# A recurrent attention followed by two mixtures on one core: seven token blocks instead of eight in the first mixture, a bit-narrowing in two passes, sums moved between engines, and a new order of the first steps

## The chip, the cores and the metric

The kernel runs on 1 core of a Trainium2 chip. The metric is the device time of the program in microseconds (us): the median of several runs, and beside it the time of one profiled execution, whose trace is read here. TensorE (PE in the profile) multiplies matrices, VectorE (DVE), ScalarE (ACT) and GpSimd (POOL) work element by element, and SyncE (SP) issues the DMAs. Each engine works through its own list of instructions in order; semaphores hold an instruction back until what it needs is there.

## The reference

```python
for t in range(S):                                   # 4 batches, 8 heads, S = 768, D = 48
    cur = np.einsum('bhd,bhe->bhde', u[None] * kt, vt)
    y[:, :, t] = np.einsum('bhd,bhde->bhe', rt, state + cur)
    state = wt[:, :, :, None] * state + np.einsum('bhd,bhe->bhde', kt, vt)
x = y as (3072 tokens, 384)
h = x @ w_in;  g = h * sigmoid(1.702 h);  x = g @ w_out          # first mixture, 384 -> 2048 -> 384
h = x @ w_in2; s = h * softmax(h)                                # second mixture, 384 -> 1024 -> 384
out = (layer_norm(s) * g_ln) @ w_out2
```

The weights of both mixtures arrive as 64-bit floats and are made 32-bit floats on the chip. Every product of a mixture is made of three matrix multiplications (high times high, high times low part, low times high), each at the short float format of the PE.

## The kernel before

The 3072 tokens are 24 units of 128. A unit's attention is a chain over several engines: cumulative products of the decays on DVE (`f_scan`, then `f_back`), scaled r and k (`f_r0` and `f_k` on DVE, `f_r1` on POOL), scores on PE (`scores`), a mask on DVE (`masked`), the new state on PE and DVE (`states`, `update`), the result on PE (`mix`), the bonus term (`bonus` on POOL, `bonus_sum`, then `bonus_mul` on POOL), the sum with it (`total`), and the turned copy that the mixture reads, as a high and a low part (`turn`, `out_hi`, `out_lo`). Each unit needs the state of the one before it.

The first mixture goes over blocks of units (`BLOCKS`) and over 16 slices f of its hidden size. A slice of a block is a rise (`rise`, 9 multiplications of 128x128 weights with all tokens of the block), two gelus on ACT (`gelu`), a low part on DVE (`rest`) and a fall (`fall`, 9 multiplications into three accumulators). A multiplication streams 128 columns for each unit of the block. The results of a rise stand in two banks of PSUM by turns, and a bank is free again after the block's `rest`.

The weights of slice f are loaded raw (`load1`), narrowed from 64 to 32 bits in passes by `narrow` (one on ACT, the others on DVE), and split into a high and a low part (`split1`). The weights of the second mixture are narrowed by the same function beside the last block.

The order of everything up to the third or fourth block is written out by hand in `START`, a string of tokens that is worked through from left to right. In it `F1` to `F5` are the first steps of a unit, `SA`, `M0`, `M1`, `DA`, `DB`, `D`, `U1`, `U2` scores, masks, states and updates, `B` the bonus products, `BR` its sum, `BV` its product, `X`, `V`, `T`, `O`, `OL` the result, its sum, its turning and its two parts; `N0` to `N3` the passes of the narrowing, `H` and `C` the split of a weight slice; `h`, `e`, `g`, `o` rise, gelu, rest and fall of block and slice. A star puts a step that DVE would do on PE and ACT (for `V`, `OL` and `C`: PE subtracts or adds through a multiplication with the unit matrix, ACT copies). After START the tables `VISITS`, `ENTRY`, `SHORT` and `LONG` say at which slice of which block the remaining units' steps are issued. From unit `LONE` on, a unit's result is turned by two trips through DRAM instead of by PE. In the end the second mixture goes over units; `xsplit` makes the two parts of a unit's input.

Of the kernel before, what the change touches and what calls it, by code (L numbers as in the profile page):

```python
# [46 lines left out]
V:2* g0:1 N3:3 Lw:6 C:2* N1:4 h0:2 T:2 F5:3 N2:4 H:3 C:3 La:3 N0:5 N1:5 o0:0 O:2 h0:3 e0:2 N3:4 Lw:7 ST:3 N2:5 F1:4
g0:2 BR:3 OL:2* SA:3 M1:3 SK:3 e0:3 DA:3 U1:3* o0:2 M0:3 DB:3 F2:4 g0:3 H:4 C:4 N0:6 La:4 N0:7 U2:3* N1:6 N3:5 N2:6
N1:7 Lrkw:5 BV:3 X:3* Lb:4 N3:6 h0:4 V:3* Lw:8 T:3 O:3 e0:4 H:5 o0:1 N2:7 OL:3* g0:4 o0:3 Lw:9 h1:0 e1:0 F3:4 N3:7
h1:1 F5:4 o0:4 g1:0 F4:4 Lw:10 N0:8 Ln:4 C:5 H:6 N1:8 e1:1 g1:1 N0:9 N1:9 C:6 H:7 C:7 o1:0 h1:2 N2:9 e1:2 SA:4 g1:2  # L50
ST:4 h1:3 e1:3 U2:5 SK:4 o1:1 h1:4 B:4 g1:3 N3:9 o1:3 Lw:12 N0:10 M1:4 M0:4 e1:4 g1:4 N1:10 h0:5 Lrkw:6 N2:8 N2:10
BR:4 BV:4 N3:10 e0:5 g0:5 o1:4 h1:5 e1:5 g1:5 D:4 o1:2 N0:12 h1:6 U1:4 e1:6 o0:5 H:9 H:10 h1:7 N3:8 Lw:11 Lw:13 X:4
g1:6 Lb:5 Ln:5 N1:12 F1:6 H:8 o1:6 h0:6 e1:7 N2:12 e0:6 g1:7 h0:7 N0:11 o1:7 e0:7 o1:5 U2:4 F4:6 N3:12 g0:6 o0:6 F1:5
C:8 g0:7 h1:8 e1:8 h0:8 e0:8 V:4 T:4 F2:6 F2:5 C:9 o0:7 O:4 g1:8 h0:9 F3:5 OL:4 La:5 g0:8 N1:11 e0:9 g0:9 C:10 Lw:15
N2:11 F5:5 H:12 o1:8 h1:9 h0:10 N3:11 e1:9 g1:9 o0:8 e0:10 o0:9 C:12 g0:10 N0:13 ST:5 H:11 o1:9 SK:5 N1:13 h1:10 e1:10
C:11 Lw:14 h0:11 N2:13 g1:10 F4:5 B:5 F3:6 o0:10 N0:14 N1:14 h0:12 SA:5 e0:12 e0:11 N3:13 g0:11 g0:12 N2:14 N0:15 D:5
# [13 lines left out]
VISITS = (1, 6, 10, 14, 18, 22, 26) + tuple(range(32, 64, 4))  # L70
# [3 lines left out]
    "nat+3 r0+2",  # L74
    "states+1 v2+2 updates+1 place+2 scan+3 back+3 k+3 sendk+3",
    "hi lo",
)
SHORT = (
    "scores+1 states+1 mix rk+3 total send v+2 v2+2 vd+1 fetch masks+1 w+4",
    "updates+1 r1+2 sum+1 bonus+2",  # L80
    "mul+1 nat+3 place+2 r0+2 scan+3",
    "back+3 k+3 sendk+3",
# [900 lines left out]
```

## Time and profile before

| | |
|---|---|
| median of 3 runs | 709.71 us (709.21 to 710.52) |
| profiled execution, its own time | 710.13 us |
| span from the first to the last instruction in it | 708.4 us |
| busy in the span: PE, DVE, ACT, POOL | 687.4, 553.1, 304.5, 145.4 us |
| granted clock of PE | 1.0 of full speed in all 40 slices of the span |
| first rise of block 0; first rise of block 3 (the first of three units) | 36.98 us; 174.29 us |

Busy time of PE is that of a pipeline: it shows that PE had work in flight, not that it ran at its peak. How fast it goes is read from the starts of one multiplication after the other, so in the chain that ended last as a piece's length over its number of multiplications. The profiled execution is 0.42 us above the median of the runs.

### The profile page before, as it was taken

How to read it: one execution, taken by the hardware profiler on the slowest of the kernel's cores; microseconds unless marked ns; L12 is line 12 of the kernel's file. 1: busy time of each engine (PE TensorE's matmuls, PEld its weight loads, DVE VectorE, ACT ScalarE, POOL GpSimd, SP SyncE). 2: the span in 40 equal slices, each digit the busy share in tenths (PEclk: the TensorE clock that was granted, in tenths of full speed). 3: DMA queues.
4: the chain of work that ended last, by engine and by line, in shares of the span. 5: the costliest groups of instructions: out<-in, count | busy, mean ns of one | idle time of the engine just before them, and what ended most of it. 6: DMA issues, size and time to landing. Idle time of an engine off the chain costs nothing.

```text
span 708.4 us, 16384 instructions
## 1 busy us (share of the span) xinstructions
PE 687.4 (97%) x6541; PEld 614.1 (87%) x6541; DVE 553.1 (78%) x898; ACT 304.5 (43%) x617; POOL 145.4 (21%) x144
## 2 busy tenths in 40 slices
PE   2899999999999999999999999999999999999997
PEld 2678999999999999988878888888889979999997
DVE  8799999888899999577777532687688878888872
ACT  2356554433233333323333223556655554545552
POOL 5431322343223232122322100120000000000000
PEclk9999999999999999999999999999999999999999
DMA  7668533433456567544444212332145544444443
GB/s 267 243 201 261 179 132 107 143 86 113 132 147 193 154 166 209 169 120 120 123 146 124 85 34 80 101 108 68 60 147 161 166 153 159 142 142 155 156 146 112
DMA packets 69292, 101.11 MB, mean 143 GB/s; under 512 B 15840, under 2 KB 53984, under 8 KB 69216
## 3 DMA queue, kind: packets, MB, share of 16 engines
q1 hardware_dynamic: 69072, 99.97, 45.9%
q8 instruction: 51, 0.84, 0.5%
q14 instruction: 25, 0.20, 0.1%
q10 hardware_dynamic: 144, 0.10, 0.0%
HBM read 76.38 MB, written 23.66 MB: 141 GB/s over the span
## 4 chain that ended last, share of the span: by engine, by line
PE 91%; DVE 3%; DMA 2%; ACT 1%; issue 1%; SPq 1%; ACTq 0%; DVEq 0%
PE acc L622 27%; PE h L597 27%; PE o L733 14%; PE right L665 8%; PE left L665 6%; PE att L364 2%; PE att L274 1%; PE att L365 1%; DMA yd<-x2b 1%; PE d L519 1%; DVE w L192 1%; PE att L235 1%; DVE P L171 1%; PE att L267 1%; PE att L395 0%
## 5 line engine op out<-in xcount | busy, mean ns | idle before, releaser
L622 PE MATMUL acc<-gh,w 128*128 128x256 f32 (+2 forms) x768 | 210.7, 339 | 0.0
L597 PE MATMUL h<-xTh,w 128*128 128x256 f32 (+2 forms) x768 | 173.7, 337 | 0.0
L605 ACT ACTIVATE gh<-h 128x256 fp32r<-128x256 f32 (+2 forms) x128 | 62.8, 491 | 228.8 <-PE h L597 220.5
L622 PEld LDWEIGHTS acc<-gh,w 128*128 128x128 f32 x768 | 136.5, 189 | 12.4
L597 PEld LDWEIGHTS h<-xTh,w 128*128 128x128 f32 x768 | 128.4, 189 | 12.0 <-ACT w L521 0.5
L622 PE MATMUL acc<-gl,w 128*128 128x256 f32 (+2 forms) x384 | 128.9, 336 | 0.0
L612 DVE TENSOR_TENSOR gl<-h,gh 128x256 fp32r<-128x256 f32 (+2 forms) x128 | 70.5, 552 | 72.7 <-ACT h L607 71.5
L597 PE MATMUL h<-xTl,w 128*128 128x256 f32 (+2 forms) x384 | 87.5, 336 | 0.1
L622 PEld LDWEIGHTS acc<-gl,w 128*128 128x128 f32 x384 | 72.7, 189 | 5.5
L733 PE MATMUL o<-w,qh 128*128 128x384 f32 x384 | 70.9, 336 | 0.0
L597 PEld LDWEIGHTS h<-xTl,w 128*128 128x128 f32 x384 | 64.7, 189 | 6.2 <-DVE xTl L415 0.5
L733 PEld LDWEIGHTS o<-w,qh 128*128 128x128 f32 x384 | 67.7, 188 | 1.6
L607 ACT ACTIVATE h<-h 128x256 f32<-128x256 f32 (+2 forms) x128 | 62.4, 488 | 0.0
L710 POOL TENSOR_TENSOR sm<-sm,mhalf 128x1 f32<-128x1 f32 x24 | 13.2, 549 | 200.3 <-DVE sm L709 187.1
L177 POOL TENSOR_TENSOR R<-rk,P 64x512 f32<-64x512 f32 x24 | 31.2, 1302 | 89.4 <-PE att L365 45.8
L665 PE MATMUL right<-w,x2h 128*128 128x512 f32 x156 | 40.0, 392 | 0.9 <-ACT x2h L653 0.9
L206 POOL TENSOR_TENSOR nr<-nr,nk 128x384 f32<-128x384 f32 x24 | 29.3, 1219 | 52.0 <-DMA nk<-in_nat 51.8
L286 DVE TENSOR_TENSOR R<-att,cc 64x256 f32<-64x256 f32 (+1 forms) x82 | 36.8, 448 | 1.2 <-PE att L277 0.2
L224 POOL TENSOR_TENSOR vd<-vd,dg 128x384 f32<-128x384 f32 x14 | 14.0, 1001 | 114.4 <-DMA vd<-in_vn 55.1
L733 PE MATMUL o<-w,ql 128*128 128x384 f32 x192 | 37.1, 334 | 0.0
L665 PEld LDWEIGHTS right<-w,x2h 128*128 128x128 f32 x156 | 29.1, 188 | 6.8 <-ACT x2h L653 1.2
L665 PE MATMUL left<-w,x2h 128*128 128x512 f32 x132 | 33.8, 392 | 0.0
(192 smaller groups left out, 1222.6 us busy)
## 6 DMA issues: line engine op xcount, KB each, us to landing
rk<-in_rkw SPq DMA_DIRECT2D x24, 512.0 KB, 4.2
d<-t SPq DMA_DIRECT2D x24, 512.0 KB, 2.6
back<-d SPq DMA_DIRECT2D x96, 128.0 KB, 2.9
x2b<-in_w SPq DMA_DIRECT2D x11, 768.0 KB, 5.7
w<-in_rkw SPq DMA_DIRECT2D x24, 261.0 KB, 3.1
nr<-in_nat SPq DMA_DIRECT2D x24, 192.0 KB, 3.1
nk<-in_nat SPq DMA_DIRECT2D x24, 192.0 KB, 3.0
vs<-in_vn SPq DMA_DIRECT2D x48, 96.0 KB, 4.1
```

Source lines behind the costliest of these rows:

```text
L177: (e or self.nc.gpsimd).tensor_tensor(out=heads(R1[0:64]), in0=heads(s["rkw"][0:64, 0:HC]), in1=heads(s["P"])[0:64, :, 0:C], op=ALU.mult)
L206: g.tensor_tensor(out=s["nr"], in0=s["nr"], in1=s["nk"], op=ALU.mult)
L224: nc.gpsimd.tensor_tensor(out=heads(s["vd"]), in0=heads(s["vd"]), in1=dg.unsqueeze(2).to_broadcast([128, H, D]), op=ALU.mult)
L286: self.nc.vector.tensor_tensor(out=heads(R[q:q + 64])[:, h:h + n], in0=a, in1=m.unsqueeze(1).to_broadcast([64, n, C]), op=ALU.mult)
L364: mm(out=y[h][t:t + 32], lhsT=s["R0"][0:112, w], rhs=s["vs0"][0:112, e], start=one, stop=one or h == 7, tile_position=(0, t))
L597: nc.tensor.matmul(out=h_ps, lhsT=W1[f][:, ws + c * 128:ws + (c + 1) * 128], rhs=xs[:, c, tok], start=n == 0, stop=n == 8)
L605: nc.scalar.activation(out=gh, in_=h_ps, func=AF.Gelu_apprx_sigmoid)
L607: return nc.scalar.activation(out=h_ps, in_=h_ps, func=AF.Gelu_apprx_sigmoid)
L612: nc.vector.tensor_tensor(out=gl_, in0=g, in1=gh.bitcast(F32), op=ALU.subtract)
L622: nc.tensor.matmul(out=a, lhsT=W1[f][:, ws + e * 128:ws + (e + 1) * 128], rhs=gs, start=first and n == 0, stop=last and n == 2)
L665: nc.tensor.matmul(out=h_ps[:, b * 512:(b + 1) * 512], lhsT=xs[:, c], rhs=W2I[c][wb][:, b * 512:(b + 1) * 512], start=n == 0 and c == 0, s ...
L733: nc.tensor.matmul(out=o, lhsT=(lo if n == 2 else hi)[:, f * 128:(f + 1) * 128], rhs=W2O[f][n == 1], start=n == 0 and f == 0, stop=n == 2 ...
```

## The change

- `BLOCKS` has seven blocks: 2, 2 and five times 4 units (before: 2, 2, 2, 3, 3 and three times 4). START now ends behind the first two rises of the third block; the remaining slices of that block belong to the loop that follows, with units 8 to 11 attended beside it. The loop has 64 slices before and after.
- `narrow` has one pass less on DVE. The ACT pass now also makes the sign (a leaky function with a large negative slope), DVE shifts the low words in place, and one DVE pass joins the two.
- The bonus sum of units 0 to 8 is done on ACT, as eight accumulating copies of 48 columns each (`BS`); the bonus product of units 6 and 8 too, as eight scaled copies (`BX`). The other sums stay on DVE.
- Three memsets at the start move from DVE to POOL, and one that stood between steps of unit 0 moves to the start.
- Starred steps: `C:2`, `V:2`, `V:3`, `OL:0` and `OL:2` lose the star, `OL:6` and `OL:7` get it.
- Units 3, 4, 6 and 8 load their v once more (`Lv`), as one tile, in START.
- `LONE` is 9, and unit 11 is turned by PE.
- In the second mixture `xsplit` of the next unit is issued one step earlier where two units are begun in one step.

```diff
-LONE = 10
+LONE = 9
-BLOCKS = [(0, 2), (2, 2), (4, 2), (6, 3), (9, 3), (12, 4), (16, 4), (20, 4)]
+BLOCKS = [(0, 2), (2, 2), (4, 4), (8, 4), (12, 4), (16, 4), (20, 4)]
 START = """
-Lrkw:0 F1:0 F3:0 F2:0 F4:0 F5:0 SA:0 Lrkw:1 F1:1 F3:1 Ln:0 Lcst ST:0 B:0 Lw:1 N0:1 M1:0 F5:1 M0:0 La:0 Ln:1 F4:1 F2:1
+Lrkw:0 Lrkw:1 F1:0 F3:0 F2:0 Ln:0 Lcst B:0 F1:1 F5:0 F4:0 SA:0 Lw:1 Lb:0 ST:0 La:0 Lw:0 F3:1 SK:0 Ln:1 M0:0 DA:0 F4:1
...
-VISITS = (1, 6, 10, 14, 18, 22, 26) + tuple(range(32, 64, 4))
+VISITS = (1, 5, 8) + tuple(range(12, 64, 4))
...
-        v.memset(self.ipc, 0.0)
-        for t in self.vs1:
-            v.memset(t[32:64], 0.0)
+        for t in (self.ipc, self.vs1[0][32:64], self.vs1[1][32:64]):
+            self.nc.gpsimd.memset(t, 0.0)
+        v.memset(self.vs0[0][64:112], 0.0)
...
-    def bonus_sum(self, i):
+    def bonus_sum(self, i, e=None):
...
-        self.nc.vector.reduce_sum(out=s["dg"], in_=heads(s["nr"]), axis=AX.X)
+        if e is None:
+            self.nc.vector.reduce_sum(out=s["dg"], in_=heads(s["nr"]), axis=AX.X)
+            return
+        for h in range(H):
+            x = s["nr"][:, h * D:(h + 1) * D]
+            e.activation(out=x, in_=x, func=AF.Copy, accum_out=s["dg"][:, h:h + 1])
...
-    def narrow(raw, t, steps=(0, 1, 2, 3)):
+    def narrow(raw, t, steps=(0, 1, 2)):
...
-            nc.scalar.activation(out=t.bitcast(F32), in_=Hw.bitcast(F32), func=AF.Copy, scale=2.0 ** -112)
+            nc.scalar.activation(out=t.bitcast(F32), in_=Hw.bitcast(F32), func=AF.Prelu, scale=2.0 ** -112, alpha=-(2.0 ** 32))
         if 1 in steps:
-            nc.vector.tensor_scalar(out=t, in0=t, scalar1=3, scalar2=0x7FFFFFFF,
-                                    op0=ALU.logical_shift_left, op1=ALU.bitwise_and)
+            nc.vector.tensor_scalar(out=L, in0=L, scalar1=29, scalar2=None, op0=ALU.logical_shift_right)
         if 2 in steps:
-            nc.vector.scalar_tensor_tensor(out=t, in0=Hw, scalar=0x80000000, in1=t, op0=ALU.bitwise_and, op1=ALU.bitwise_or)
-        if 3 in steps:
-            nc.vector.scalar_tensor_tensor(out=t, in0=L, scalar=29, in1=t, op0=ALU.logical_shift_right, op1=ALU.bitwise_or)
+            nc.vector.scalar_tensor_tensor(out=t, in0=t, scalar=3, in1=L, op0=ALU.logical_shift_left, op1=ALU.bitwise_or)
...
-            if nx < min((new[0] if new else NU) + 2, NU):
+            if nx < min((new[-1] if new else NU) + 2, NU):
                 xsplit(nx)
```

Two places of the instruction lists show what the new START moves. The first is DVE's list at the first two weight slices. Before, from `f_r0` of unit 1 to the update of unit 1's state (L479, L482 and L484 are the passes of the narrowing, L213 the bonus sums of units 0 and 1, L345 updates, L286 a mask):

```order
L183 TENSOR_TENSOR R_1_170<-rk_138,P_140 48x512
L479 TENSOR_SCALAR x2a<-x2a 128x768
L213 TENSOR_REDUCE dg_190<-nr_146 128x8
L345 TENSOR_TENSOR vs_0_92<-att_83,pc_111 48x384
L213 TENSOR_REDUCE dg_231<-nr_166 128x8
L482 SCALAR_TENSOR_TENSOR x2a<-x2b,x2a 128x768
...
L482 SCALAR_TENSOR_TENSOR x2a<-x2b,x2a 128x768
L484 SCALAR_TENSOR_TENSOR x2a<-x2b,x2a 128x768
L286 TENSOR_TENSOR R_1_172<-acc_79,cc 64x512
L484 SCALAR_TENSOR_TENSOR x2a<-x2b,x2a 128x768
L345 TENSOR_TENSOR vs_1_93<-acc_78,pc_142 48x384
```

Now, from the same step of unit 1 on (L485 is the shift, L487 the joining pass, L351 updates, L292 masks):

```order
L180 TENSOR_TENSOR R_1_182<-rk_112,P_130 48x512
L485 TENSOR_SCALAR x2b<-x2b 128x768
L196 TENSOR_TENSOR rk_112<-rk_112,w_110 112x512
L351 TENSOR_TENSOR vs_0_92<-att_83,pc_116 48x384
L292 TENSOR_TENSOR R_0_120<-att_84,cc 64x512
L487 SCALAR_TENSOR_TENSOR x2a<-x2a,x2b 128x768
L351 TENSOR_TENSOR vs_1_91<-att_83,pc_116 48x384
...
L168 SCALAR_TENSOR_TENSOR P_235<-w_209,ind 112x520
L292 TENSOR_TENSOR R_1_184<-acc_79,cc 64x512
L351 TENSOR_TENSOR vs_1_93<-acc_78,pc_161 48x384
```

Between the two state updates of unit 0 and that of unit 1 stand two narrowing passes a slice instead of three, no bonus sum, and the scan of unit 2, which before came behind the update.

The second place is PE's list around the first rise of block 0 (the rise is the row that writes `h_0`; L419 and L420, now L425 and L426, are the low part of unit 1's input, L235, now L241, turns k of unit 2). Before:

```order
L395 MATMUL acc_78<-cc,vd_336 128x128 x3
L419 MATMUL acc_78<-cc,vd_336 128x128 x3
L420 MATMUL acc_78<-xTh_71,neg 128x384
L235 MATMUL att_83<-cc,rk_313 128x112 x4
L597 MATMUL h_0_409<-xTh_71,w_0_295 128x256 x3
L597 MATMUL h_0_409<-xTl_72,w_0_295 128x256 x3
L308 MATMUL att_83<-vs_0_90,cc 48x192 x2
```

Now:

```order
L401 MATMUL acc_78<-cc,vd_356 128x128 x3
L241 MATMUL att_83<-cc,rk_211 128x112 x4
L273 MATMUL att_84<-R_2_365,rk_211 64x64
...
L314 MATMUL att_83<-vs_0_90,cc 48x192 x2
L322 MATMUL att_83<-vs_0_90,kTs_433 48x48
...
L425 MATMUL acc_78<-cc,vd_356 128x128 x3
L426 MATMUL acc_78<-xTh_73,neg 128x384
L600 MATMUL h_0_451<-xTh_73,w_0_317 128x256 x3
L600 MATMUL h_0_451<-xTl_74,w_0_317 128x256 x3
```

The scores of unit 2 and the first half of its state (L273 and L314, L322), which stood behind the first rise, stand ahead of it now. ACT's whole list has four table loads before and four now.

## Rows read from the trace of the kernel before

**Rows 1.** Windows: stretch, length, then busy us of PE, PEld, DVE, ACT, POOL.

```profile
0.00:37.00 37.00, 22.22 (x315) 15.89 (x315) 30.88 (x41) 10.08 (x20) 16.39 (x18) 1.00 0.75 252
37.00:65.00 28.00, 27.73 (x401) 22.79 (x399) 26.98 (x39) 16.82 (x34) 9.76 (x8) 1.00 0.69 221
65.00:130.00 65.00, 65.00 (x810) 63.77 (x809) 62.61 (x101) 33.79 (x79) 17.69 (x13) 1.00 0.48 156
130.00:174.30 44.30, 43.85 (x699) 42.45 (x698) 37.25 (x66) 15.98 (x46) 19.35 (x19) 1.00 0.34 99
```

**Rows 2.** Groups by line and form, PE: rises with the high part of the input.

```profile
L597 PE MATMUL h<-xTh,w 128*128 128x512 f32 x288 | 81.1, 390 | 0.0
L597 PE MATMUL h<-xTh,w 128*128 128x256 f32 x288 | 48.9, 285 | 0.0
L597 PE MATMUL h<-xTh,w 128*128 128x384 f32 x192 | 43.6, 334 | 0.0
```

**Rows 3.** Chain that ended last, in order of time: start, length, what.

```profile
64.58 2.16 PE h L597 x18
201.07 1.56 PE h L597 x9
306.68 2.04 PE h L597 x9
```

**Rows 4.** Timeline of PE around the first rises: start, length, what.

```profile
36.98 0.60 PE L597 MATMUL h<-xTh,w 128*128 128x256 f32 x3
38.65 0.85 PE L308 MATMUL att<-vs,cc 112*48 112x192 f32 x4 [0.27 <-ACT kTs L240]
...
40.86 0.91 PE L519 MATMUL d<-x2a,cc 128*128 128x384 f32 x2
...
45.07 0.91 PE L358 MATMUL att<-vd,cc 128*128 128x384 f32 x2
45.91 0.23 PE L364 MATMUL att<-vs,R 112*32 112x48 f32 x1
46.73 0.91 PE L519 MATMUL d<-x2a,cc 128*128 128x384 f32 x2
...
48.47 0.54 PE L597 MATMUL h<-xTh,w 128*128 128x256 f32 x3
...
52.05 0.55 PE L235 MATMUL att<-cc,rk 112*128 112x112 f32 x4
52.44 0.85 PE L419 MATMUL att<-cc,vd 128*128 128x128 f32 x6
...
53.39 0.27 PE L267 MATMUL att<-R,rk 48*64 48x64 f32 x1
```

**Rows 5.** Timeline of DVE, narrowing passes and one bonus sum.

```profile
15.62 1.24 DVE L479 TENSOR_SCALAR x2a<-x2a 128x768 uint32<-128x768 uint32 x1
16.79 0.54 DVE L213 TENSOR_REDUCE dg<-nr 128x8 f32<-128x384 f32 x1
...
18.42 1.53 DVE L482 SCALAR_TENSOR_TENSOR x2a<-x2b,x2a 128x768 uint32<-128x768 uint32 x1
...
21.88 1.64 DVE L482 SCALAR_TENSOR_TENSOR x2a<-x2b,x2a 128x768 uint32<-128x768 uint32 x1
23.55 0.96 DVE L484 SCALAR_TENSOR_TENSOR x2a<-x2b,x2a 128x768 uint32<-128x768 uint32 x1
...
34.23 0.54 DVE L479 TENSOR_SCALAR x2a<-x2a 128x768 uint32<-128x768 uint32 x1
```

**Rows 6.** Timeline of POOL beside the pass at 21.88.

```profile
21.50 1.19 POOL L207 TENSOR_TENSOR nr<-nr,cc 128x384 f32<-128x384 f32 x1
```

**Rows 7.** Timeline of PE in the second mixture, with the wait behind the release sign.

```profile
579.62 1.66 PE L665 MATMUL right<-w,x2h 128*128 128x512 f32 x6 [0.91 <-ACT x2h L653]
```

**Rows 8.** Groups by line and form, ACT: a small copy and an accumulator read.

```profile
L256 ACT ACTIVATE kTs<-x2b 128x64 f32<-128x64 f32 x13 | 3.2, 243 | 0.0
L684 ACT ACTIVATION_READ_ACCUMULATOR e<-c 128x1 f32 x24 | 4.5, 186 | 0.0
```

More of the change, by code (lines that the diff above doesn't have):

```diff
@@ L47 @@
[L47 to L56, printed above, removed]
@@ L73 @@
     "scan+2 back+2 k+2 w+4 sendk+2 r1+2 sum+1 mul+1 bonus+2",
[L74 to L82, printed above, removed]
+    "states+1 v2+2 nat+3 updates+1 r0+2",
+    "place+2 scan+3 back+3 k+3 sendk+3",
     "hi lo",
@@ L89 @@
     "hi lo back+3 k+3 sendk+3",
+)
+BYPE = (
+    "scores+1 states+1 mix rk+3 total v+2 v2+2 masks+1 w+4",
+    "r1+2 updates+1 sum+1 bonus+2",
+    "flip vd+1 mul+1 hi lo r0+2 nat+3 place+2 scan+3",
+    "back+3 k+3 sendk+3",
 )
@@ L158, in load_v @@
             self.nc.sync.dma_start(out=s["vs1"][64:128], in_=self.vn[i, 64:128])
-            if i % UB == 0:
+            if i and i % UB == 0:
                 self.nc.vector.memset(s["vs0"][64:112], 0.0)
@@ L218, in load_vd, with bonus_mul @@
         self.nc.sync.dma_start(out=vd, in_=self.vn[i])
[L220 removed]
+    def bonus_mul(self, i, e=None):
         nc, ap, s = self.nc, self.ap, self.st[i]
[L222 to L229 removed]
+        dg, g = s["dg"], nc.gpsimd
+        if e is not None:
+            for h in range(H):
+                x = s["vd"][:, h * D:(h + 1) * D]
+                e.activation(out=x, in_=x, func=AF.Copy, scale=dg[:, h:h + 1])
+        elif "vd" in s:
+            g.tensor_tensor(out=heads(s["vd"]), in0=heads(s["vd"]), in1=dg.unsqueeze(2).to_broadcast([128, H, D]), op=ALU.mult)
+        else:
+            vd = s["vd"] = ap.tile([128, HD], F32, tag="vd", name=f"vd{i}", bufs=VDB)
+            for q, vt in ((0, s["vs0"]), (64, s["vs1"])):
+                g.tensor_tensor(out=heads(vd[q:q + 64]), in0=heads(vt[q:q + 64]),
+                                in1=dg[q:q + 64].unsqueeze(2).to_broadcast([64, H, D]), op=ALU.mult)
     def turn_k(self, i):
@@ L574, in upto @@
                 elif part == 2:
-                    narrow(*T[m], (1, 2, 3))
+                    narrow(*T[m], (1, 2))
                 else:
@@ L765, in steps @@
             masks=masks, updates=updates, sum=at.bonus_sum, mul=at.bonus_mul, bonus=at.bonus, r0=at.f_r0, r1=at.f_r1,
-            scan=at.f_scan, back=at.f_back, k=at.f_k, sendk=at.send_k, place=at.place_k, turn=at.turn_k, copy=at.copy_k)
-        G = [[] for _ in range(NF1 * (LAST - 3))]
+            scan=at.f_scan, back=at.f_back, k=at.f_k, sendk=at.send_k, place=at.place_k, flip=at.turn, turn=at.turn_k, copy=at.copy_k)
+        G = [[] for _ in range(NF1 * (LAST - 2))]
         for n, t in enumerate(VISITS):
-            for m, line in enumerate(ENTRY if n == 0 else SHORT if t < 2 * NF1 else LONG):
+            for m, line in enumerate(ENTRY if n == 0 else BYPE if n == 3 else LONG):
                 for op, _, i in (x.partition("+") for x in line.split()):
@@ L795, in rwkv_moe_moe2 @@
             elif op[0] == "o":
-                fall(int(op[1]), int(i), t in (falls[0], "o2:0"), t == falls[-1])
+                fall(int(op[1]), int(i), t == falls[0], t == falls[-1])
             elif op[0] in "heg":
@@ L801, in rwkv_moe_moe2 @@
     with tc.manual_schedule():
-        pend += [(2, NF1 - 2), (2, NF1 - 1)]
+        pend += [(2, 0), (2, 1)]
         plan = steps()
-        for j in range(3, LAST):
+        for j in range(2, LAST):
             for f in range(NF1):
-                hstep(j, f)
-                for g in plan[16 * (j - 3) + f]:
+                if (j, f) > (2, 1):
+                    hstep(j, f)
+                for g in plan[16 * (j - 2) + f]:
                     g()
```

49 lines of the change are left out of this document (23 added, 26 removed).

## Prediction, on record before the changed kernel ran

> **What bounds the kernel now.** I read the windows of the start first. From 65 us on PE is busy in all of its time, and what it does there is the mixture with the attention between; DVE is busy for 62.6 of the 65 us up to 130 us, and for 37.3 of 44.3 behind that [rows 1]. So there are two engines to watch: PE, whose work is the time from the first rise on, and DVE, which has almost no room in the first stretch and so decides whether PE gets its input. Up to the first rise at 36.98 us PE mostly waits: 22 of 37 us busy, with few instructions in it.
>
> How fast PE goes shows in the chain that ended last, where rises follow without a gap: 2.16 us for 18 multiplications of 256 columns, 1.56 for 9 of 384, 2.04 for 9 of 512 [rows 3]. That is 0.120, 0.1733 and 0.2267 us each. From one to the next, 128 columns cost 0.0533 us, and 0.0133 us is left over for each multiplication, however wide. The busy means of the groups (285, 334, 390 ns [rows 2]) are time in flight and hide this.
>
> **Fewer, wider multiplications.** The groups have 288, 192 and 288 rises with the high part [rows 2]; those with the low part are half as many and the falls are as many again, so the mixture has 864 of 256, 576 of 384 and 864 of 512 columns: 103.7 + 99.8 + 195.9 = 399.4 us. With two blocks of two and five of four units it has 576 and 1440: 69.1 + 326.4 = 395.5 us. The streamed columns are the same; 288 starts fall away. **-3.8 us**, and no cover can take it back while PE is the bound.
>
> **What PE does besides, behind the first rise.** From the timeline, as distances between starts [rows 4]: a starred split of a weight slice costs 48.47 - 46.73 = 1.7 us, and `C:2` goes to DVE: -1.7. A starred sum costs 45.91 - 45.07 = 0.8, and two go: -1.7. A starred low part costs 53.39 - 52.44 = 0.95; `OL:2` goes, `OL:6` and `OL:7` come: +0.95. The turning of one unit's k (52.05 to 52.44) goes: -0.4. Scores and first half state of unit 2 (38.65 to 40.86) move ahead of the first rise: -2.2. Sum **-5.1 us**.
>
> **The first rise.** The way to it runs through DVE's list, of which order and prices are known. For the first two weight slices DVE spent 1.24 + 1.53 + 1.64 + 0.96 us on the passes shown, and two more like them, about 7 us, and 1.1 on two bonus sums before the update of unit 1's state [rows 5]. Now there are two shifts and two joining passes: 2 x (0.54 to 1.24) + 2 x (0.96 to 1.64) = 3.0 to 5.8 us, and no sum. DVE is lighter by 2.3 to 5.1; I take the middle, 3.8, since POOL is as busy there as before. Against it: the scan of unit 1, about as long as that first contended shift, 1.2 us, now stands ahead of unit 0's scores, and PE does the 2.2 us of unit 2 first, but no longer the 0.95 us of `OL:0`. So 36.98 - 3.8 + 1.2 + 2.2 - 0.95 = 35.7 us (34.3 to 37.1): **-1.3 us**.
>
> The three memsets that go to POOL are hidden: POOL has 16.4 us of work in 37 us [rows 1], and DVE's first scan waits for a load meanwhile. The pass on ACT keeps its size and I leave its price; the list of ACT has four table loads, as before. The five extra loads of v are 192 KB each among 252 GB/s already moved in the first 37 us; at that rate one takes 0.8 us, and none stands ahead of the first rise in SP's list.
>
> **The second mixture.** PE waits 0.91 us for the high part of a unit's input where two units are begun in one step [rows 7]. The copy is issued a step earlier now: **-0.9 us**, or nothing if ACT is late there for another reason. The narrowing beside the last block gets cheaper on DVE too, worth nothing: PE has work there without a gap.
>
> **The sums on ACT.** Eight copies and eight accumulator reads: 8 x (0.243 + 0.186) = 3.4 us a unit from the nearest rows, 1.9 if every read hides behind the next copy [rows 8]; the scaled products the same without the read. No trace shows the form itself. Behind the first rise that is six sums and two products, 14 to 24 us. ACT was busy 16.8 of 28 us and 33.8 of 65 us there [rows 1], so it has the room; what it costs if a sum stands ahead of a gelu is the second rival.
>
> **DVE against PE up to the third block.** This is the term with the least certainty. Between the first rise and the first rise of block 3 before, 174.3 - 37.0 = 137.3 us passed, and DVE was busy for 27.0 + 62.6 + 37.3 = 126.8 us of them [rows 1]. Off PE's side come the third block (288 x 0.12 = 34.6) and most of the 5.1 above, so PE needs about 100 us. Off DVE's side come one pass for each of 14 slices (14 x 0.96 = 13.4), seven sums (3.8) and 16 rests of 256 columns (no row is shown; under the 0.54 us of the bonus sum [rows 5], so about 7): it needs about 102 us, and it has to be through before the third rise of block 2, which wants a bank that the rest of the first gives back. DVE falls behind PE by 2 us, and by 5 with the gaps of 4% that it has at its fullest [rows 1]. It starts ahead, because it is lighter up to the first rise. I take a new wait of **+3 us** there (0 to 6). Beyond it a block of four units gives DVE more time for a unit than one of three did, so it catches up and I expect PE without gaps.
>
> The price of the shift is in this term. It reads and writes every second word in place, and no row shows that; the old shift of the same size took 0.54 us on packed words, a pass with two inputs 0.96 [rows 5]. I take the former, as the same instruction with one input; the other end is the first rival.
>
> **The rule that speaks against it.** In the trace two passes that ran while POOL worked took 1.53 and 1.64 us, against 0.96 for one right behind, when POOL's product of 21.50 to 22.69 was over [rows 5, 6]. The Trainium skill, SBUF — State Buffer, section Who interferes with whom, says why: VectorE and GpSimd share a port pair as an exclusive lock, for VectorE instructions with two SBUF inputs and for one-input ones in a two-port mode; whoever starts first blocks the other. By that rule both remaining passes stay exposed to POOL, and the trace agrees as far as these rows go. It is the third rival's mechanism.
>
> **Sum.** 710.13 - 3.8 - 5.1 - 1.3 - 0.9 + 3 = 702.0 us for the profiled execution. That one was 0.42 us above its median, so **701.6 us** as a median.
>
> **Rivals.**
> 1. *DVE becomes the bound of the start.* The shift costs 0.96 instead of 0.54: 14 x 0.42 = 5.9 us more on DVE behind the first rise, all of it in front of the third block. 707.5 us. For it: DVE at 96% in the fullest stretch. Against: the old shift's 0.54. Chance 0.22.
> 2. *ACT holds back the banks.* A sum waits for POOL's product and then takes 3.4 us, with a gelu behind it. Rise and fall of the other bank cover 2.2 us; six exposed sums cost 6 x 1.2 = 7.2. 708.8 us, no change that can be told. For it: ACT works strictly in order. Against: 40 to 48% of its time is free. Chance 0.08.
> 3. *Slower: VectorE and GpSimd block each other.* If every pass of the 14 slices ran at its contended price, 1.24 + 1.64 instead of 0.54 + 0.96, DVE would need 19.3 us more: 721 us. Over 711.1 us it comes from 9.5 us on, so when half of the slices are hit. For it: both early passes were hit. Against: POOL was busy in 9.8 of 28 and 17.7 of 65 us [rows 1], so about a third should be hit, and some of that is in the prices already. Chance 0.07.
> 4. *The start fills better than I think*: first rise at 34.3, no new wait: 710.13 - 3.8 - 5.1 - 2.7 - 0.9 - 0.4 = 697.2 us. Chance 0.06.
>
> **How the numbers follow.** The forecast, PE bound with a wait of 0 to 6 us before the third block, has 0.57; its own range is 698.5 to 705. With the first rival's 0.22 and part of the fourth the range is 697.5 to 707.5; left out are the second and third rival and the ends, about 0.2. What a measurement of this kernel can tell from no change is 0.2%, so 708.3 to 711.1 us. Faster: forecast, first and fourth rival less a little of the first's upper end, 0.87; no change: most of the second and that end, 0.06; slower: the third, 0.07.
>
> **What would show it.** The first rise at 35.7 us (34.3 to 37.1); rises of 512 columns at 2.04 us for 9; the shift at 0.54 to 0.62 us, the joining pass at 0.96; the bonus sum on ACT 1.9 to 3.4 us for eight copies; PE waiting for a rest of block 2 near 136 us for 0 to 6 us and for nothing afterwards; no wait of 0.9 us in the second mixture. Waits of PE on ACT's gelus spread over 40 to 130 us would mean the second rival, joining passes of 1.5 us the third. The forecast is wrong if DVE's list is behind PE's over the whole of the first two blocks, for then its sum and not PE's makes the time.

## The result and the profile after

The median is 698.66 us (698.41 to 699.90, 4 runs); the kernel before, on the same chip, had 709.78 us (709.21 to 710.52, 4 runs). The ratio is 0.9846, with a 95% interval of 0.9829 to 0.9863. Forecast were 701.6 us, 697.5 to 707.5: the time lies in the range, 2.9 us below the number.

The profiled execution took 698.77 us with a span of 697.0. The windows of the start, to be read against [rows 1] (stretch, length, busy us of PE, PEld, DVE, ACT, POOL with instructions, granted clock of PE, DMA share, GB/s):

```profile
0.00:37.00 37.00, 23.49 (x372) 16.67 (x372) 31.91 (x40) 17.71 (x72) 20.88 (x24) 1.00 0.84 298
37.00:65.00 28.00, 27.35 (x383) 24.65 (x382) 26.26 (x41) 20.60 (x55) 8.22 (x7) 1.00 0.75 242
65.00:130.00 65.00, 64.15 (x971) 61.88 (x973) 59.73 (x99) 37.97 (x144) 17.52 (x17) 1.00 0.49 160
```

DVE is still nearly full, though a little less than before (26.26 of 28 and 59.73 of 65 us; 26.98 and 62.61 before), PE too, and ACT has 38.3 us of work up to 65 us instead of 26.9. The timeline of PE at the first rise of block 0, the first and third rise of block 2 (L600 is the rise) and the last rise of all (a row ends with the wait before it, where there was one), to be read against [rows 4]:

```profile
34.70 0.51 PE L600 MATMUL h<-xTh,w 128*128 128x256 f32 x3
...
130.87 0.94 PE L600 MATMUL h<-xTh,w 128*128 128x512 f32 x3
...
139.85 0.98 PE L600 MATMUL h<-xTh,w 128*128 128x512 f32 x3
...
490.01 0.84 PE L600 MATMUL h<-xTh,w 128*128 128x512 f32 x3
```

The last rise of the kernel before started at 499.95 us, and its span was 708.36 to two decimals (now 696.99). So three stretches share the gain: up to the first rise 36.98 - 34.70 = 2.28 us, from there to the last rise 462.97 - 455.31 = 7.66, behind it 208.41 - 206.98 = 1.43; together 11.4 us, and what lies around the span is 1.8 us in both.

What PE waited for from the first rise to 140 us, all of it (instruction and its releaser, us in total, times, longest):

```profile
PE att L280 <- DVE P L348: 0.5, 1, 0.5
PE h L600 <- ACT xTl L427: 0.5, 2, 0.2
PE att L314 <- ACT kTs L246: 0.3, 1, 0.3
PE att L306 <- DVE R L292: 0.2, 1, 0.2
```

No rise waits for a rest of the slice before, and nothing waits for a gelu; what is left is 1.5 us in five pieces. The new operations, in the groups of DVE and ACT (out<-in, form, count, busy us, mean ns, idle time before):

```profile
L487 DVE SCALAR_TENSOR_TENSOR x2a<-x2a,x2b 128x768 uint32<-128x768 uint32 x9 | 9.1, 1010 | 0.2
L485 DVE TENSOR_SCALAR x2b<-x2b 128x768 uint32<-128x768 uint32 x11 | 6.8, 616 | 0.1
L485 DVE TENSOR_SCALAR x2a<-x2a 128x768 uint32<-128x768 uint32 x5 | 2.8, 556 | 0.1
...
L215 ACT ACTIVATE nr<-nr 128x48 f32<-128x48 f32 x72 | 16.3, 232 | 1.8 <-POOL nr L204 1.8
L215 ACT ACTIVATION_READ_ACCUMULATOR nr<-nr 128x1 f32 x72 | 13.8, 191 | 0.0
```

The shift (L485) has the price taken for it, 0.56 to 0.62 us, the joining pass (L487) about 1.0. A bonus sum is at the low end: its eight pairs start 0.225 us apart (14.74 to 16.45 us for the first unit), 1.9 us in all. In the second mixture no wait of PE stands in the trace from the last rise on, where [rows 7] had 0.91 us.

### The profile page after: what moved, and what is told of

Its sections match the earlier page's. It is cut to its first block, busy times and chain, and to the rows that moved or that the text cites. A ratio compares the mean times of both kernels' runs of the same rounds, so it can differ in the third digit from the quotient of the medians.

```text
span 697.0 us, 15809 instructions
## 1 busy us (share of the span) xinstructions
PE 678.2 (97%) x6239; PEld 583.6 (84%) x6239; DVE 524.4 (75%) x841; ACT 316.4 (45%) x739; POOL 139.4 (20%) x140
## 4 chain that ended last, share of the span: by engine, by line
PE 90%; DVE 3%; ACT 1%; DMA 1%; issue 1%; POOL 0%; SPq 0%; ACTq 0%; POOLq 0%; DVEq 0%
PE acc L625 27%; PE h L600 27%; PE o L736 14%; PE right L668 8%; PE left L668 7%; PE att L370 2%; PE att L280 1%; PE att L371 1%; PE att L273 1%; DVE w L189 0%; PE att L307 0%; DVE R L292 0%; PE att L241 0%; DMA kd<-x2b 0%; DMA x2b<-kd 0%
## 5 line engine op out<-in xcount | busy, mean ns | idle before, releaser
L625 PE MATMUL acc<-gh,w 128*128 128x512 f32 (+1 forms) x672 | 202.4, 363 | 0.0
L600 PE MATMUL h<-xTh,w 128*128 128x512 f32 (+1 forms) x672 | 168.0, 360 | 0.0
L608 ACT ACTIVATE gh<-h 128x512 fp32r<-128x512 f32 (+1 forms) x112 | 59.9, 535 | 229.2 <-PE h L600 220.8
L625 PEld LDWEIGHTS acc<-gh,w 128*128 128x128 f32 x672 | 121.7, 189 | 19.9
L615 DVE TENSOR_TENSOR gl<-h,gh 128x512 fp32r<-128x512 f32 (+1 forms) x112 | 68.2, 610 | 90.4 <-ACT h L610 89.4
L600 PEld LDWEIGHTS h<-xTh,w 128*128 128x128 f32 x672 | 117.0, 189 | 19.2 <-ACT w L524 0.2
L625 PE MATMUL acc<-gl,w 128*128 128x512 f32 (+1 forms) x336 | 120.7, 359 | 0.0
L600 PE MATMUL h<-xTl,w 128*128 128x512 f32 (+1 forms) x336 | 84.6, 360 | 0.5 <-ACT xTl L427 0.5
L600 PEld LDWEIGHTS h<-xTl,w 128*128 128x128 f32 x336 | 58.6, 189 | 11.0 <-ACT xTl L427 0.9
L610 ACT ACTIVATE h<-h 128x512 f32<-128x512 f32 (+1 forms) x112 | 59.6, 532 | 0.0
L668 PE MATMUL right<-w,x2h 128*128 128x512 f32 x156 | 39.9, 391 | 0.0
L292 DVE TENSOR_TENSOR R<-att,cc 64x256 f32<-64x256 f32 (+1 forms) x82 | 36.7, 448 | 1.1
L736 PE MATMUL o<-w,ql 128*128 128x384 f32 x192 | 37.1, 334 | 0.0
L168 DVE TENSOR_TENSOR_SCAN P<-w,ind 112x520 f32<-112x520 f32 x24 | 34.8, 1448 | 1.9 <-DMA w<-in_rkw 1.5
L189 DVE TENSOR_TENSOR_SCAN w<-w,ipc 112x520 f32<-112x520 f32 x24 | 34.9, 1454 | 0.8
```

The source lines that it names most:

```text
L168: self.nc.vector.tensor_tensor_scan(out=P, data0=s["w"][:, 0:H * PW], data1=self.ind[:, 0:H * PW], initial=0.0, op0=ALU.mult, op1=ALU.add)
L189: v.tensor_tensor_scan(out=w[:, n:0:-1], data0=w[:, n:0:-1], data1=self.ipc[:, n:0:-1], initial=0.0, op0=ALU.mult, op1=ALU.add)
L292: self.nc.vector.tensor_tensor(out=heads(R[q:q + 64])[:, h:h + n], in0=a, in1=m.unsqueeze(1).to_broadcast([64, n, C]), op=ALU.mult)
L600: nc.tensor.matmul(out=h_ps, lhsT=W1[f][:, ws + c * 128:ws + (c + 1) * 128], rhs=xs[:, c, tok], start=n == 0, stop=n == 8)
L608: nc.scalar.activation(out=gh, in_=h_ps, func=AF.Gelu_apprx_sigmoid)
L610: return nc.scalar.activation(out=h_ps, in_=h_ps, func=AF.Gelu_apprx_sigmoid)
```

## The experiments

All but one are the kernel after with one edit. They are compared with 698.66 us, and stretches of their traces with those above. The kernel before, run beside each group of them, had medians of 709.76 to 710.90 us, so medians of two groups tell differences from about 1 us on; traces of like code agree to 0.1 us from the first rise to the first of block 2. Behind that they can differ: the kernel after and that of experiment 2 are alike up to the last rise and lie 0.95 us apart between first and last rise.

The first rise itself came between 33.9 and 34.8 us in five kernels that are alike up to it. A race sets which: POOL's first bonus product waits for a load, and a product of DVE that stands beside it is held up where POOL was first. The kernel after, and then that of experiment 2:

```profile
8.96 0.99 POOL L203 TENSOR_TENSOR nr<-nr,nk 128x384 f32<-128x384 f32 x1 [1.58 <-DMA nk<-in_nat]
9.10 1.40 DVE L180 TENSOR_TENSOR R<-rk,P 48x512 f32<-48x512 f32 x1
```

```profile
9.07 1.55 POOL L203 TENSOR_TENSOR nr<-nr,nk 128x384 f32<-128x384 f32 x1 [1.72 <-DMA nk<-in_nat]
9.07 0.69 DVE L180 TENSOR_TENSOR R<-rk,P 48x512 f32<-48x512 f32 x1
```

With DVE's product at 1.37 to 1.50 us the first rise came at 34.69 to 34.84 (the kernel after, experiments 1 and 7), with 0.69 at 33.92 and 34.03 (experiments 2 and 8). A first rise is to be set beside one with the same outcome of this race.

**1. The starts of multiplications** (`a_halves`).

```diff
-        for ws, xs in ((0, XH), (0, XL), (768, XH)):
...
+        for s in (slice(0, 256), slice(256, 512)) if j in (4, 5) else (slice(0, TB),):
+            n = 0
+            for ws, xs in ((0, XH), (0, XL), (768, XH)):
```

> The kernel after with the rises of two of the blocks of four units (blocks 4 and 5) done in two halves of 256 columns: 288 matrix multiplications more, the same columns, nothing else changed. By the price of a start read from the chain before, 0.0133 us, 3.8 us more: 702.5 us, and 18 multiplications of 256 columns in 2.16 us instead of 9 of 512 in 2.04. Rival: a start is hidden where PE has no gap, and the term of -3.8 is none: 698.7 us.

Measured: 702.28 us (701.65 to 702.52), 3.6 more. The first rise stood at 34.69 us, the last at 493.73, 3.72 us later than in the kernel after. The chain that ended last, start and length of one rise:

```profile
303.57 2.15 PE h L602 x18
```

The 0.0133 us a start (with the load of its weights) are real and not hidden: 3.72 us over 288 is 0.0129. The term of -3.8 us is right.

**2. The input of the second mixture** (`a_xsplit_old`).

```diff
-            if nx < min((new[-1] if new else NU) + 2, NU):
+            if nx < min((new[0] if new else NU) + 2, NU):
```

> The kernel after with the old line for the second mixture's input, new[0] instead of new[-1]. By the prediction's term the wait of 0.9 us where two units are begun in one step comes back and the time is 699.6 us. If that wait had gone for another reason (the other order ahead of it): no change, 698.7 us. From the last rise to the end the kernel after is 1.37 us shorter than the one before; if all of that is the line, 700.0 us.

Measured: 700.46 us (700.32 to 700.73), 1.8 more. The last rise stood at 490.18, within 0.2 us of the kernel after; behind it 208.3 us passed instead of 207.0. (The first rise had been 0.78 us earlier, by the race above, but the third of block 2 stood at 139.82 us, in the kernel after at 139.85: in between an update on DVE took 1.30 us beside POOL instead of 0.55, and PE waited 0.48 us behind it.) The timeline of PE has the wait again:

```profile
569.89 1.66 PE L668 MATMUL right<-w,x2h 128*128 128x512 f32 x6 [0.91 <-ACT x2h L656]
```

So the line alone is worth 1.3 us, and all of it arises here: counted from the last rise, this trace and that of the kernel after lie 0.01 us apart up to this group; the group starts 1.1 us late, and it and the next one each take about 0.1 us longer. The granted clock stays at 1.00, so that the wait of 0.91 costs 1.3 us is not the clock; what else it is was not tried.

**3. The old narrowing** (`a_old_narrow`), its last two passes together at the place of the joining pass.

```diff
-            nc.scalar.activation(out=t.bitcast(F32), in_=Hw.bitcast(F32), func=AF.Prelu, scale=2.0 ** -112, alpha=-(2.0 ** 32))
+            nc.scalar.activation(out=t.bitcast(F32), in_=Hw.bitcast(F32), func=AF.Copy, scale=2.0 ** -112)
...
-            nc.vector.tensor_scalar(out=L, in0=L, scalar1=29, scalar2=None, op0=ALU.logical_shift_right)
+            nc.vector.tensor_scalar(out=t, in0=t, scalar1=3, scalar2=0x7FFFFFFF,
+                                    op0=ALU.logical_shift_left, op1=ALU.bitwise_and)
         if 2 in steps:
-            nc.vector.scalar_tensor_tensor(out=t, in0=t, scalar=3, in1=L, op0=ALU.logical_shift_left, op1=ALU.bitwise_or)
+            nc.vector.scalar_tensor_tensor(out=t, in0=Hw, scalar=0x80000000, in1=t, op0=ALU.bitwise_and, op1=ALU.bitwise_or)
+        if 2 in steps:
+            nc.vector.scalar_tensor_tensor(out=t, in0=L, scalar=29, in1=t, op0=ALU.logical_shift_right, op1=ALU.bitwise_or)
```

> The kernel after with the old narrowing: ACT copies, DVE makes three passes instead of two (second and third behind one another at the place of the joining pass). On DVE that is 0.96 us more for each of two slices ahead of the first rise and 14 behind it. Theory 1 (DVE's list decides the time up to the third block, as the term of +3 in the prediction has it): 1.9 + 13.4 = 15.3 us more, 714 us, a first rise at 36.6 and PE waiting for rests all through the first two blocks. Theory 2 (PE decides, DVE has room behind the first rise): the first rise alone moves, 1.9 us, 700.6 us, and DVE is busy for about 73 of 65 + 8 us without PE waiting longer.

Measured: 715.72 us (715.15 to 718.56), 17.1 more, as theory 1 has it. First rise at 35.60, first of block 2 at 146.05, so 110.5 us between them instead of 96.2. Waits of PE from 30 to 140 us:

```profile
PE h L603 <- DVE gl L618: 3.8, 5, 2.5
PE att L318 <- DVE vs L351: 2.1, 1, 2.1
PE att L401 <- DVE vs L351: 1.2, 1, 1.2
...
PE h L603 <- DVE w L529: 0.7, 1, 0.7
```

Rises wait for rests (`gl`) and for low parts of weights (`w`). With these passes DVE decides. About 1.7 of these 14.3 us more are PE's clock, as an estimate from the granted 0.58 and 0.57 from 40 to 44 us. The order of START needs the new narrowing; it was not arranged anew for the old one.

**4. The same part alone** (`b_two_pass`): the kernel before with the edits of `narrow` from the change's diff, step 2 empty and the joining pass in step 3, everything else as it was.

> The kernel before with one part of the change alone, the narrowing in two passes on DVE (its order, blocks and sums stay). DVE is lighter by 0.96 us for each slice, two ahead of the first rise and 14 behind it. If DVE's list decided the kernel before too, as it does the kernel after with the old narrowing: up to 15 us less, 695 us. If PE decides it (DVE was given its relief by starred steps on PE, and its idle time behind the first rise was 10.5 of 137 us): the first rise alone, 2 to 4 us less, 706 to 708 us. I expect the second.

Measured: 710.63 us (709.01 to 711.67), beside 710.27; ratio 1.0004, 0.9990 to 1.0018. No change can be told. In its profiled execution, the shortest of twelve, the first rise stood at 35.05 us, 1.9 earlier; the windows from the first rise to the first of block 3, the kernel before and then this one:

```profile
37.00:174.30 137.30, 136.58 (x1905) 129.01 (x1903) 126.84 (x204) 66.59 (x159) 46.80 (x40) 1.00 0.48 151
```

```profile
35.10:172.40 137.30, 136.51 (x1903) 128.95 (x1902) 116.25 (x191) 66.38 (x159) 43.65 (x40) 1.00 0.47 150
```

DVE has 10.6 us less to do and the stretch is the same to 0.1 us (137.31 and 137.39). PE alone decided it. Later 0.7 us of the 1.9 is given back: a state waits 1.36 instead of 0.72 us for a load of v at 197 us. Why the median does not show the rest is open.

**5. A narrowing that leaves out the low words** (`a_drop3`).

```diff
-            nc.vector.tensor_scalar(out=L, in0=L, scalar1=29, scalar2=None, op0=ALU.logical_shift_right)
...
-            nc.vector.scalar_tensor_tensor(out=t, in0=t, scalar=3, in1=L, op0=ALU.logical_shift_left, op1=ALU.bitwise_or)
+            nc.vector.tensor_scalar(out=t, in0=t, scalar1=3, scalar2=None, op0=ALU.logical_shift_left)
```

> The kernel after with a narrowing that leaves the low words out: no shift, and a shift of one input in place of the joining pass, so the three lowest bits of every narrowed weight are zero. It takes 0.56 + 0.42 us a slice off DVE, 2.0 ahead of the first rise and 13.7 behind it, and adds nothing elsewhere. It asks what PE alone would allow. If DVE's list decides the kernel after by a little (the wait of 0 to 6 us in the prediction, taken as 3) and moves the first rise: 3 to 6 us less, 693 to 696 us. If DVE decides it by much: up to 13 us less, 685 us. If PE decides it alone: the first rise, 2 us at most, 697 us.

Measured: 698.90 us (697.92 to 701.55). The windows from the first rise to the first of block 2, the kernel after and then this one:

```profile
34.70:130.90 96.20, 94.47 (x1393) 88.84 (x1392) 88.99 (x143) 60.68 (x202) 27.78 (x26) 1.00 0.57 187
```

```profile
36.80:132.90 96.10, 94.78 (x1393) 89.14 (x1391) 77.53 (x128) 60.43 (x202) 27.70 (x26) 1.00 0.54 183
```

11.5 us less on DVE, and the stretch shrinks by 0.1. The first rise was not earlier here: it came at 36.75. With the lighter list DVE and ACT ran into loads, and PE waited behind ACT:

```profile
32.67 1.24 DVE L168 TENSOR_TENSOR_SCAN P<-w,ind 112x520 f32<-112x520 f32 x1 [2.42 <-DMA w<-in_rkw]
31.93 0.89 ACT L483 ACTIVATE x2a<-x2b 128x768 f32<-128x768 f32 x1 [2.15 <-DMA x2b<-in_w]
33.30 0.85 PE L314 MATMUL att<-vs,cc 112*48 112x192 f32 x4 [1.47 <-ACT kTs L246]
```

The DMA engines were busy for all of 28 to 34 us (share 0.98 to 1.05), and PE's clock then stood at 0.56 and 0.59 of full speed from 34 to 38 us. So behind the first rise DVE's list does not hold PE back in the kernel after. Ahead of it, in this trace, the loads stand right behind DVE's list, and less work on DVE alone did not bring the first rise forward.

**6. The shift in two steps** (`a_shift_twice`).

```diff
-            nc.vector.tensor_scalar(out=L, in0=L, scalar1=29, scalar2=None, op0=ALU.logical_shift_right)
+            nc.vector.tensor_scalar(out=L, in0=L, scalar1=14, scalar2=None, op0=ALU.logical_shift_right)
+            nc.vector.tensor_scalar(out=L, in0=L, scalar1=15, scalar2=None, op0=ALU.logical_shift_right)
```

> The kernel after with the shift of the narrowing made in two steps, by 14 and by 15 bits: one more DVE instruction of 0.56 to 0.62 us for each slice, 1.1 us ahead of the first rise and 8.1 behind it. It is the first rival of the prediction (a dearer shift) made real and somewhat larger. If DVE's list decides up to the third block: 9.2 us more, 708 us, and PE waits for rests. If DVE has room there: the first rise, 1.1 us, 700 us. The granted clock of PE is to be looked at where PE runs dry.

Measured: 705.56 us (705.36 to 707.55), 6.9 more. First rise at 35.66, 1.0 later than in the kernel after and 1.7 later than in experiment 2, where DVE's early product took 0.69 us too; first of block 2 at 137.44, so 101.8 us between them, 5.6 more than in the kernel after. Of 8.1 us put on DVE (14 times 0.58, as priced) 2.5 are taken up. In the kernel after PE decides, with DVE that close behind.

**7. Stars put back** (`a_stars`), in START:

```diff
-BV:2 C:2 Ln:3 X:2 Lrkw:4 C:1* h0:1 V:2
+BV:2 C:2* Ln:3 X:2* Lrkw:4 C:1* h0:1 V:2*
...
-OL:2
+OL:2*
```

> The kernel after with the stars put back on C:2, X:2, V:2 and OL:2, so that PE and ACT do what DVE does now: PE has 1.7 + 0.85 + 0.95 = 3.5 us more, DVE 0.96 + 0.55 + 0.55 = 2.1 us less. If PE decides there: 702.2 us. If DVE decides with room on PE: 696.6 us. If both are level, as the prediction has it: the 3.5 us of PE less some of DVE's 2.1, 700 to 702 us.

(`X` and `V` carry their stars together; the kernel before had all four.) Measured: 702.53 us (702.14 to 703.48), 3.9 more; first rise at 34.84, first of block 2 at 134.05, 99.2 us between them, 3.0 more for the 3.5 us put on PE. Work put on PE is paid nearly in full, although DVE gets lighter.

**8. More stars taken off** (`a_fewer_stars`), at three places of START:

```diff
-OL:3*
+OL:3
...
-OL:6*
+OL:6
...
-OL:7*
+OL:7
```

> The kernel after with three more stars taken off: OL:3, OL:6 and OL:7 go from PE and ACT to DVE. PE has 3 x 0.95 = 2.85 us less, DVE 3 x 0.55 = 1.65 us more behind the first rise. The run with the shift in two steps put 8.1 us on DVE there and the stretch from the first rise to the third block's grew by 5.5, so DVE has about 2.6 us to spare. If that room serves wherever it is used: 2.85 us less, 695.8 us. If DVE is late at the two places (near 72 and near 125 us), part of it comes back as waits for rests: 697 to 698.7 us.

Measured: 701.94 us (701.37 to 702.27), 3.3 more. The timeline of PE at the first rise of block 1, which reads unit 3's low part, and windows behind it:

```profile
54.82 0.52 PE L600 MATMUL h<-xTh,w 128*128 128x256 f32 x3
57.97 0.62 PE L600 MATMUL h<-xTl,w 128*128 128x256 f32 x3 [2.63 <-DVE xTl L421]
```

```profile
56.00:58.00 2.00, 0.03 (x1) 0.03 (x1) 1.97 (x4) 0.00 (x0) 0.00 (x0) 1.00 0.75 206
58.00:60.00 2.00, 2.00 (x12) 2.00 (x13) 0.97 (x2) 0.66 (x2) 0.00 (x0) 0.69 1.01 395
60.00:62.00 2.00, 2.00 (x12) 2.00 (x12) 1.82 (x4) 1.02 (x3) 0.82 (x1) 0.50 0.51 141
62.00:64.00 2.00, 2.00 (x18) 2.00 (x18) 1.50 (x3) 2.00 (x4) 1.64 (x2) 0.96 0.04 8
```

The low part (`xTl`) stands in DVE's list behind other work (DVE is busy for 1.97 of 2 us), PE waits 2.63 us for it, and then PE's clock is at 0.69 and 0.50 of full speed for about four us. DVE's room is not at this place. A star does more than move work: it takes one step out of a full list. How much each of the three stars is worth was not tried apart.

**9, 10, 11. The bonus sums back on DVE**, all of units 0 to 8 (`a_sums_dve`), then units 2 to 8 (`a_sums_late`) and units 0 and 1 (`a_sums_front`) apart: `BS` becomes `BR` in START, as with

```diff
-F2:1 N0:1 BS:0 N1:1 BV:0 F5:1 B:1 U1:0* ST:1
+F2:1 N0:1 BR:0 N1:1 BV:0 F5:1 B:1 U1:0* ST:1
```

> The kernel after with the bonus sums of units 0 to 8 as one reduction on DVE (0.54 us each) instead of eight accumulating copies on ACT. Theory 1 (DVE decides up to the third block): two sums ahead of the first rise 1.1 us, six behind it 3.2 us, together 4.3: 703.0 us. Theory 2 (PE decides): 1.1 us at the first rise and no more: 699.8 us. The second rival of the prediction, reversed (the sums on ACT hold back gelus): no slower than 698.7 us, and fewer waits of PE on ACT between 40 and 130 us.

Measured: 707.37 us, and 703.41 to 713.27 over twelve runs; the kernel after spans 1.5 us. The run of 703.41 had a mean granted clock of 1.000, the three of 709.6 to 713.3 one of 0.988 to 0.990. Windows of the profiled execution (709.59 us), whose first rise came at 39.9:

```profile
26.00:28.00 2.00, 1.01 (x20) 0.56 (x17) 1.94 (x4) 0.59 (x3) 1.63 (x1) 1.00 1.02 424
28.00:30.00 2.00, 0.90 (x2) 0.30 (x2) 1.94 (x3) 0.67 (x1) 1.85 (x3) 0.91 1.02 406
30.00:36.00 6.00, 5.23 (x105) 4.48 (x105) 5.94 (x8) 2.24 (x4) 0.28 (x1) 0.50 0.84 323
36.00:40.00 4.00, 4.00 (x29) 3.11 (x29) 1.67 (x4) 0.00 (x0) 0.03 (x1) 0.51 0.69 205
```

PE was busy for 1.9 of 4 us, then its clock was 0.5 for ten, which is the 1.2 GHz level. Then it is DVE that waits for PE: of 4 us from 36 on it works 1.67.

> The kernel after with the bonus sums of units 2 to 8 on DVE, those of units 0 and 1 on ACT as before it. One of the seven stands ahead of the first rise (0.54 us), six behind it (3.2 us), of which 2.6 us fit into DVE's room: 1.2 us more, 699.9 us, if the clock of PE stays at 2.4 GHz. If the dear part of the run with all sums on DVE lies behind the first rise: up to 7 us more.

Measured: 704.43 us (703.44 to 709.59), 5.8 more; the expectation missed. In the profiled execution (703.44 us) the clock stayed at 1.00, the first rise stood at 34.9 and the first of block 2 at 134.97: 3.9 us longer, for 3.2 us on DVE. A rise waits 2.0 us for a rest, once, and a turning 1.5 us for a state. So DVE's 2.5 us of room, spread over 14 slices in experiment 6, are not to be had where these sums stand.

> The kernel after with the bonus sums of units 0 and 1 alone on DVE, both ahead of the first rise. As delay of DVE's list alone: 1.1 us, 699.8 us. In the run with all sums on DVE the first rise came at 39.9 instead of 34.7 us and the granted clock of PE was 0.5 from 30 to 39 us. If the two sums bring that on: the first rise at 38 to 40 us, 702 to 704 us, and times of single runs that lie 3 us and more apart.

Measured: 702.91 us, in two groups: 700.46, 700.66 and 701.21 us at a mean clock of 1.0, and 704.62, 704.74 and 706.41 at 0.992 to 0.993. Two sums of 0.55 us cost 2.0 us in the first group, and in the other half of the runs about 4 us more, with the lower clock. In the one trace, of the first group, the first rise came at 36.12, with DVE's early product at 0.69 us: 1.4 us behind the kernel after, 2.2 behind experiment 2, which had the same 0.69.

**12. A version that might beat both** (`a_pool_r0`): `f_r0` of units 2 and 3 on POOL (`F6`), and `OL:6` without its star.

```diff
-F4:2 X:1* V:1* N1:2 F5:2 N2:2 T:1 Lb:2 F2:2 ST:2
+X:1* V:1* N1:2 F5:2 N2:2 T:1 Lb:2 F2:2 F6:2 ST:2
...
-F4:3
+F6:3
...
-OL:6*
+OL:6
```

> The kernel after with two edits that make the two engines in its start lighter: the scaled r (f_r0) of units 2 and 3 goes from DVE to POOL, which is idle from 29.1 to 34.8 us (DVE 1.2 + 0.7 us less), and OL:6 alone loses its star (PE 0.95 us less, DVE 0.55 more near 122 us; OL:3, whose loss made PE wait 2.6 us and brought its clock down, and OL:7 keep theirs). Unit 2's scores wait for its k at 30.8 us; with the product on POOL the k comes 1.2 us and the r 0.5 us sooner, so the first rise comes at 34.2 instead of 34.7. If both pay: 0.5 + 0.95 us, 697.2 us. If POOL's products make DVE's passes beside them dearer (one joining pass beside POOL took 1.38 instead of 0.95 us) and OL:6 is late: 698.7 to 700 us.

Measured: 701.15 us (700.73 to 701.72), 2.5 more. The first rise came at 34.34, with DVE's early product at 0.69 us, so 0.4 later than in experiment 2 and not 0.5 sooner. The timeline of DVE beside POOL, and then of POOL:

```profile
27.76 1.11 DVE L485 TENSOR_SCALAR x2a<-x2a 128x768 uint32<-128x768 uint32 x1
28.78 1.67 DVE L196 TENSOR_TENSOR rk<-rk,w 112x512 f32<-112x512 f32 x1
```

```profile
27.25 1.17 POOL L174 TENSOR_TENSOR R<-rk,P 64x512 f32<-64x512 f32 x1
28.48 1.42 POOL L180 TENSOR_TENSOR R<-rk,P 48x512 f32<-48x512 f32 x1
```

In the kernel after the same shift took 0.56 us and the same product 0.69. DVE gave up 1.23 us and lost 1.53. The Trainium skill, SBUF — State Buffer, section Who interferes with whom, says that the engine that comes second is blocked for the whole instruction of the other. The trace agrees: shift and product end at 28.87 and 30.45 us, each about half a us behind the end of the POOL instruction beside it (28.42 and 29.90). `OL:6` gained 1.05 us at the rise in front of block 2 and lost 1.3 at the next one; late steps up to 200 us cost another 1.7, of which some may be the spread of up to 0.95 us told above. No kernel was found that beats the one after the change.

## Why the prediction was right, and where it was off

**Starts, -3.8 us: right.** 288 starts cost 3.6 us in the median and 3.72 in the trace (experiment 1). The rises of 512 columns take 2.04 us for 9, as said.

**PE's other work, -5.1 us: right in its largest part, the rest not tried.** Four of its stars, forecast at 3.5 us, cost 3.9 when put back, 3.0 of them up to block 2 (experiment 7). From the first to the last rise the gain is 7.66 us where this term and the one of the starts say 8.9; 1.2 us are unaccounted for. The 1.5 us of small waits up to 140 us would cover them, but the kernel before had small waits there too, and like code differs by up to 0.95 us in this stretch.

**The first rise, -1.3 us: under-sized, -2.28.** It came at 34.70, inside the 34.3 to 37.1. (The terms add to 35.6, not to the 35.7 that stands there.) The cheaper narrowing alone moved it by 1.9 us in the kernel before (experiment 4), and the sums taken off DVE are worth 1.4 to 2.2 in the kernel after (experiment 11); I had 3.8 for both, which these bear out, and 2.5 against them for the scan and the work of unit 2 on PE. So the 2.5 was too much; how much of it was hidden was not tried. The sum also had no term for DVE's product held up by POOL, which is 0.7 us in this trace and not in others.

**The second mixture, -0.9 us: 1.3 to 1.4.** The wait that I read went as said; it had cost 0.4 us more than its visible length (experiment 2).

**A new wait of +3 us before the third block: the step that failed.** DVE does not decide there: 11.5 us off its list brought no rise behind the first forward (experiment 5). DVE's need up to the third rise of block 2 was worked out as 102 us (its terms give 102.6), and it was busy for 97.6, for the largest part because 13 scans and not 16 fall into the stretch (17.5 us instead of 21.0). PE's was worked out as about 100 (its terms give 97.6), and it took 105.2 (34.70 to 139.85). I had taken the stretch before up to the first rise of block 3 and left out that the new one goes on through two rises of 512 columns in block 2, 4.1 us. With these two corrections the sign turns: DVE, put 2 to 5 us behind, is ahead, by the 2.5 us of experiment 6. Only at the third rise of block 2 it is level: a hold-up of 0.75 us on DVE came through to that rise in experiment 2. The time lies in the range because the range held the case of no wait, not because the wait was there. Without this term the sum is 699.0 us for an execution that took 698.8; that it fits so well is in part chance, since the other three misses, 1.0 and 0.5 us on one side and 1.2 on the other, nearly cancel.

**The rivals.** *DVE becomes the bound* fell with the shift's price, 0.56 to 0.62 us. Its mechanism is real and near: half a us more for each slice gave 6.9 us (experiment 6). *ACT holds back the banks* fell: PE waited for no gelu from the first rise to 140 us. (Taking the sums from ACT made the kernel slower, but that put them on DVE and so tests both at once.) *VectorE and GpSimd block each other* happened in places (a joining pass of 1.38 us, the early product of 1.40 us, which moves the first rise by 0.7) and costs much where POOL gets more to do (experiment 12), but the mean of the joining pass stayed at 1.0 us. *The start fills better than I think*, given a chance of 0.06, is what came nearest: no new wait, the first rise at 34.7 where it said 34.3, and 698.7 us where it said 697.2.

**What the narrowing brings** belongs to the whole, not to itself. Alone it changes nothing that can be told, because PE decided the kernel before; in the new order its absence costs 17 us, because DVE then decides (experiments 4 and 3). That the stars taken off and the shorter work on PE have brought DVE so near is argued from the rows; which part of the new order does it was not tried, and neither were `LONE`, the extra loads of v and the memsets by themselves.

## What to carry to other kernels

When two engines are level, count both over the same stretch, to the same instruction, before saying which is behind; four us left out on one side turned the sign here. Test a suspected bound by taking work off that engine as well as putting work on it: the one asks whether it decides, the other how near it is. An engine's room in sum is no room at a place: before work is moved into a list that is full, look at which later instruction waits for the next entry in it. And when work is taken off, look at what stands next behind it; here it was the loads.

## What the runs showed of the hardware

- **A gap of PE can be paid a second time, through the clock.** After a wait of 2.63 us the granted clock was 0.69, then 0.50, of full speed for about four us, an estimated 1.6 us of work lost by these shares; after 1.9 busy us of 4 it was 0.5 for ten, an estimated 4.6 us from the 9.2 us that PE was busy in them. The kernel before stayed at 1.00 with 0.84 busy us of 2 (34 to 36 us), and the kernel after with 1.30 and 1.38 of 2. The same kernel had a mean clock of 1.0 and of 0.992 in different executions (experiment 11). The Trainium skill, TensorE: Matmul & The Clock Gate, section HAM oscillation — how this bites in real kernels, says that waits for input bring the clock down and that the work behind them starts at the low rate; these rows agree.
- **The accumulating copy on ACT is cheap in a row.** A copy of 48 columns took 232 ns and the read of the sum 191 ns, but pairs started every 225 ns.
- **A shift in place on every second 32-bit word runs at the price of one on packed words**, 0.56 to 0.62 us for 768 elements where the old one took 0.54, and POOL's products hold it up, to 1.11 us.
- **Which of DVE and POOL starts a product first can be a matter of a load, and worth 0.7 us**: 0.69 or 1.40 us for the same instruction on DVE, where POOL's product started at the same time or 0.14 us before it.
